# DeltaNet and MLP-Mixer on one core: the joins of 32-blocks on eight 32x32 places of TensorE instead of four

## The chip, the core and the metric

The kernel runs on one core of a Trainium2 chip. TensorE does the matmuls (PE in the profile; its weight loads are listed apart as PEld), VectorE is DVE, ScalarE is ACT, GpSimd is POOL, and SyncE (SP) issues the DMAs. TensorE takes its operands from SBUF and writes to PSUM; the copies that this text speaks of bring results from PSUM back to SBUF on ACT. The metric is the device time of one execution in microseconds (us), lower is better.

## What is computed

A DeltaNet attention over 4 batches, 8 heads, 768 positions and 48 features, then an MLP-Mixer block on its output. All in fp32.

```python
def _attn_ref(q, k, v, beta):
    k_n = k / (np.linalg.norm(k, axis=-1, keepdims=True) + 1e-06)
    state = np.zeros((B, H, D, D), dtype=np.float32)
    for t in range(S):
        kt, vt, bt = (k_n[:, :, t], v[:, :, t], beta[:, :, t, None])
        y[:, :, t] = np.einsum('bhd,bhde->bhe', q[:, :, t], state)
        v_old = np.einsum('bhde,bhd->bhe', state, kt)
        state = state + bt[:, :, :, None] * np.einsum('bhd,bhe->bhde', kt, vt - v_old)

def _moe_ref(x, w_tok1, w_tok2, w_ch1, w_ch2):
    xt = x.transpose(0, 2, 1)
    h = np.maximum(xt @ w_tok1, 0.0) @ w_tok2
    u = x + h.transpose(0, 2, 1)
    return u + np.maximum(u @ w_ch1, 0.0) @ w_ch2
```

## The kernel before

The recurrence runs over chunks of C = 64 positions. A *unit* u is 128 positions of one batch, two chunks; there are 24 units, 6 to a batch. Within a chunk the recurrence is a triangular system for each head, so the kernel makes the inverse of a 64x64 unit triangular matrix per head and chunk. A unit has 8 such pairs of matrices (`NB = 8`, index `nb = 2p + cc` for head pair `p` and chunk `cc`); each pair stands on the 128 partitions, one matrix on partitions 0 to 63 and the other on 64 to 127. They are the columns `TC` of the unit's tile `gm`.

The inverse is made in blocks of HB = 32: the two diagonal 32x32 blocks of each matrix are inverted by `invert` (on DVE, in rounds of units: 0 to 3, 4 and 5, 6 to 9, 10 to 13, 14 to 17, 18 to 21, 22 and 23; from unit 6 on the blocks go out and come back by DMA, `to_parts` and `from_parts`). The block off the diagonal is then two 32x32 products, and that is `join` (line 726):

- DVE transposes the first inverted block into `t11` (line 734).
- TensorE multiplies it with the block off the diagonal into `p_z` (line 748), ACT copies `p_z` to `zst` (line 754).
- TensorE multiplies `zst` with the second inverted block into `p_x`, and ACT copies `p_x` into `gm` (`into`, line 739).

From unit 6 on the second product of a unit is done together with the first product of the next unit of its round: that is a *double join* (lines 748 and 751, 32 matmuls in turn, four copies). The first unit of a round has the first product alone; the last one also has its own second product behind it, a *closing join* (line 767, 16 matmuls, two copies). Double joins are those of units 7, 8, 9, 11, 12, 13, 15, 16, 17, 19, 20, 21 and 23, closing ones those of units 9, 13, 17, 21 and 23 (units 0 to 5 are done one by one).

A matmul whose operands lie on 32 partitions and whose result goes to 32 partitions uses one of the array's 32x32 places: the row block is given by the operands' partitions, the column block by the result's. With

```python
halves = [(slice(r.start, r.start + HB), slice(r.start + HB, r.stop)) for r in PAR]
```

row blocks 0 and 2 feed column blocks 1 and 3 in the first product, row blocks 1 and 3 feed column blocks 0 and 2 in the second. So a double join uses four places, a closing join two. `p_z` and `p_x` are tiles of the PSUM tag "prep", which has two buffers that the grams `p_g` (line 440) and, for early units, the transposes `p_t` also take.

The chunks' recurrence is `recur`: `p_k` (line 790), `rest` on DVE (line 797), `p_y` and `p_w` in turn (lines 810 and 814; `p_w` reads the joined columns of `gm`), ACT's copy of `p_w` to `w_t` (line 820), `p_s` and `p_y` in turn (lines 828 and 829), DVE's `s_t` (line 837), ACT's two copies of `p_y` into `xb` (line 842). The MLP of a finished batch (`mixer`, `wide_fast`: `p_r`, `p_c`, `p_o`, `p_ut`, `p`, `p_h`) runs beside the recurrence of the next one; ACT and DVE empty its PSUM tiles (`r`, `u_t`, `xb`), tag "mlp" with three buffers.

What follows what is a table of words: every stage is a generator, and `order` names them one after the other (`j` for a join, `r` a step of the recurrence, `m` the MLP, `i` a step of `invert`, `c` and `d` the grams, `k`, `v`, `p` loads and preparation). Each word advances its generator to the next `yield`. On each engine the instructions run in this order. A join's steps are three words: the transpose, the matmuls, the copies.

Of the kernel before, what the change touches and what calls it, by code (L numbers as in the profile page):

```python
# [13 lines left out]
C = 64  # L14
U = 128
DP = 64
HB = 32
# [6 lines left out]
def kernel(  # L24
# [39 lines left out]
    nc = tc.nc  # L64
# [30 lines left out]
    def ps_prep(shape, name):  # L95
        return psum.tile(shape, FP32, name=name, tag="prep", bufs=2)
# [34 lines left out]
    NL = 2  # L131
# [208 lines left out]
        )  # L340

    ranked = set()
    spread = set()
    keyed = set()

# [26 lines left out]
    def load_kq(u):  # L372
        b, c = divmod(u, NCH)
        kst = kst_of[slot(u)]
        if u >= TU:
            yield from load_rows(u, 0, k)
            assert last_in(u) in ranked
            yield from stacked(kst, k, u)
            yield from load_rows(u, 1, q)
            return  # L380
        for pad, src in ((kpad, k), (qpad, q)):
            assert last_in(u) is None or (pad is kpad, last_in(u)) in turned
            nc.sync.dma_start(
                out=pad[slot(u)][:, :, 0:D],
                in_=src[b, :, c * U : (c + 1) * U, :].rearrange("h t d -> t h d"),
            )
            yield
            if src is k and u >= RU:
                yield from stacked(kst, k, u)

        heads = kpad[slot(u)].rearrange("t (p par) d -> t p par d", par=2)
        for cc in range(2 if u < RU else 0):
            for par in range(2):
                nc.scalar.copy(kst[PAR[par ^ cc], :, cc], heads[PAR[cc], :, par, 0:D])
                yield

    def stacked(dst, src, u):
# [55 lines left out]
    def prep(u):  # L453

        b, c = divmod(u, NCH)
        kst = kst_of[slot(u)]
        if u < TU:
            kp, qp = kpad[slot(u)], qpad[slot(u)]
        gm, kqt, nrm = gm_of(u), kqts[place(u)], nrms[place(u)]
        bet = beta_st[:, b, :, 2 * c : 2 * c + 2]  # L460

        ksq = work.tile([128, NB, D], FP32, name="ksq", bufs=1)
        nc.scalar.square(ksq, kst.rearrange("s p c d -> s (p c) d"))
        yield
        ksum = work.tile([128, NB], FP32, name="ksum")
        nc.vector.tensor_reduce(
            out=ksum, in_=ksq, axis=mybir.AxisListType.X, op=ALU.add
        )
        yield
        nrm_f = nrm.rearrange("s p c -> s (p c)")  # L470
        nc.scalar.sqrt(nrm_f, ksum)
        nc.scalar.activation(ksum, nrm_f, ACTF.Square, bias=eps)
        yield
        cs = work.tile([128, NP, 2], FP32, name="cs")
        nc.vector.reciprocal(ksum, ksum)
        nc.vector.tensor_tensor(
            out=cs, in0=ksum.rearrange("s (p c) -> s p c", c=2), in1=bet, op=ALU.mult
        )
        yield

        assert beta_in
        ps_turn = ps_mlp if u < NCH else ps_prep
        if u < TU:
            p_t = ps_turn([128, NP, 2, C], "p_t")
            for p in range(NP):
                nc.tensor.transpose(p_t[:, p], kp[:, 2 * p : 2 * p + 2], ident)
            turned.add((True, u))
            yield
            nc.scalar.copy(kqt[:, :, :, 0], p_t)
        else:  # L490
            assert (0, u) in spread and 2 * before_in(u) + 1 in keyed
            turn_rows(u, 0)
        yield
        mb = work.tile([128, NP, 2, C], FP32, name="mb", bufs=1)
        made[u] = mb
        scaler = nc.vector if u in EARLY_SC else nc.gpsimd
        scaler.tensor_tensor(  # L497
            out=mb, in0=mask_c[:, None, None, :].to_broadcast([128, NP, 2, C]),
            in1=cs[:, :, :, None].to_broadcast([128, NP, 2, C]), op=ALU.mult,
        )  # L500
        yield
        if u < TU:
            p_t = ps_turn([128, NP, 2, C], "p_t")
            for p in range(NP):
                nc.tensor.transpose(p_t[:, p], qp[:, 2 * p : 2 * p + 2], ident)
            turned.add((False, u))
            yield
            assert before_in(u) is None or before_in(u) in asked
            nc.scalar.copy(kqt[:, :, :, 1], p_t)  # L509
        else:  # L510
            assert (1, u) in spread and before_in(u) in asked
            turn_rows(u, 1)
        yield
        scaler.tensor_tensor(
            out=blocks(gm)[:, :, :, KC], in0=kst,
            in1=cs[:, :, :, None].to_broadcast([128, NP, 2, D]), op=ALU.mult,
        )
        ranked.add(u)
        grown.add(u)
        yield  # L520
# [206 lines left out]
    def join(u):  # L727

        done = joined_16 if u < NCH else inverted
        wt = gm_of(u)[:, :, TC]  # L730
        first = u < NCH or u == rounds[round_of[u][0]][0]
        last = u < NCH or u == rounds[round_of[u][0]][-1]
        assert done.issuperset([(u, 0), (u, 2)])
        nc.vector.transpose(t11, wt[:, :, 0:HB])
        yield

        def into(x, w):
            for r, r2 in halves:
                nc.scalar.copy(w[r, :, HB:C], x[r])

        assert len(left_over) == (not first)
        before = None if first else left_over.pop()
        assert first or done.issuperset([(before, 1), (before, 3)])
        p_z = ps_prep([128, NB, HB], "p_z")
        p_x = ps_prep([128, NB, HB], "p_x") if before else None
        for nb in range(NB):
            for r, r2 in halves:
                nc.tensor.matmul(p_z[r2, nb], wt[r, nb, HB:C], t11[r, nb])  # L748
                if before:
                    w = gm_of(before)[:, :, TC]  # L750
                    nc.tensor.matmul(p_x[r, nb], zst[r2, nb], w[r2, nb, HB:C])
        yield
        for r, r2 in halves:
            nc.scalar.copy(zst[r2], p_z[r2])
        if before:
            into(p_x, gm_of(before)[:, :, TC])
            joined.add(before)
        if not last:
            left_over.append(u)
        yield  # L760
        if not last:
            return
        assert done.issuperset([(u, 1), (u, 3)])
        p_x = ps_prep([128, NB, HB], "p_x")
        for nb in range(NB):
            for r, r2 in halves:
                nc.tensor.matmul(p_x[r, nb], zst[r2, nb], wt[r2, nb, HB:C])
        yield
        into(p_x, wt)
        joined.add(u)  # L770
        yield

# [92 lines left out]
    def sum_weights():  # L865
        def block_of(z):
            j, k = z
            for f in range(FT * j, FT * j + FT):
                piece_of(wc1, k, f * 128)
            return w_block(j, k)  # L870

        a = {(j, k): (j, k) for j in range(3) for k in range(NCB)}
        add, sub = ALU.add, ALU.subtract
        made = (
            ("w12", a[1, 2], a[0, 2], sub), ("w11", a[0, 1], "w12", add),
            ("w3", a[1, 0], a[0, 0], sub), ("w2", a[1, 1], "w3", sub),
            ("w5", a[1, 2], a[2, 0], add),
            ("w13", a[0, 2], a[2, 2], add), ("w14", "w13", "w5", sub),
            ("w1", a[0, 0], a[1, 2], sub), ("w13", a[2, 1], "w12", sub),
            ("w6", a[1, 0], a[1, 1], sub), ("w6", "w6", a[2, 0], add),  # L880
            ("w7", None, a[2, 0], sub),
            ("w15", a[2, 2], a[2, 1], sub), ("w15", "w15", a[1, 2], add),
            ("w9", a[0, 1], "w2", sub), ("w9", "w9", a[2, 1], add),
        )
        for i, (out, x, y, op) in enumerate(made):
            j = {"w13": 0, "w9": 0, "w1": 0, "w6": 1, "w7": 2, "w15": 2}.get(out)
            assert j is None or used.issuperset(range(FT * j, FT * j + FT))
            outs = sums[out]
            n = WB // len(outs)
            for h, o in enumerate(outs):  # L890
                cut = slice(h * n, h * n + n)
                p, q = (
                    sums[z][0][:, cut] if isinstance(z, str) else z and block_of(z)[:, cut]
                    for z in (x, y)
                )
                if p is None:
                    nc.vector.tensor_scalar_mul(o, q, -1.0)
                else:
                    nc.vector.tensor_tensor(out=o, in0=p, in1=q, op=op)
            if out not in [m[0] for m in made[i + 1 :]]:  # L900
                summed.add(out)
            yield
# [376 lines left out]
```

## Time and profile before

| | us |
|---|---|
| median of three timed runs | 641.43 (640.62 to 643.88) |
| the profiled execution's own time | 638.03 |
| its span in the trace | 636.3 |
| busy: PE / PEld / DVE / ACT / POOL | 606.3 / 529.0 / 447.3 / 259.5 / 108.7 |
| first product of joins, PE (L748, late units) | 16.2 in 704 records |
| second product in double joins, PE (L751) | 10.0 in 416 records |
| second product alone, PE (L767) | 6.2 in 288 records |
| copies zst<-p_z, ACT (L754) | 17.4 in 48 |
| copies gm<-p_x, ACT (L739) | 15.9 in 44 |

A row of the timeline gives the start and the length in us, the engine, the line, the operation, the tiles (out<-in), for matmuls the array's rows and columns, then the shape and the count of merged records; in square brackets stands how long the engine was idle before it and what ended that. A row of the groups gives line, engine, operation, tiles, shape and count, then busy us and mean ns of one, then the idle time before. A row of the stretches gives the busy us (and count) of PE, PEld, DVE, ACT and POOL, then TensorE's granted clock, the DMA share and GB/s. A record of a pipelined matmul lasts longer than the step from it to the next one; the steps between starts tell the pace.

### The profile page before, as it was taken

Reading aid. Unit: us, or ns where it says so; the run is one execution under the profiler, and the core shown is the slowest. Engines: PE = TensorE matmul, PEld = TensorE weight load, DVE = VectorE, ACT = ScalarE, POOL = GpSimd, SP = SyncE. Lnnn points to the kernel's source line nnn. Section 1 sums busy time; section 2 is a strip of 40 time slices with the busy share of each in tenths; the row PEclk is TensorE's granted clock in tenths of the full one; section 3 lists DMA queues with packets and bytes.
Section 4 is the critical chain, followed back from the end, with each engine's and each line's share of the span. In section 5 each row is a group of like instructions: output and inputs, shape, how many; then the busy total and the mean of one; then the engine's idle time right before and its main releaser. Section 6 shows DMA issues by size and latency. Waiting matters only on the chain.

```text
span 636.3 us, 21488 instructions
## 1 busy us (share of the span) xinstructions
PE 606.3 (95%) x9132; PEld 529.0 (83%) x9132; DVE 447.3 (70%) x1132; ACT 259.5 (41%) x631; POOL 108.7 (17%) x146
## 2 busy tenths in 40 slices
PE   8488798899999999999999999999999999999997
PEld 5367676667898988958999999769999987999997
DVE  4987876966899568988969987785627253373643
ACT  7758886447422242125623333135244230223240
POOL 2348364235301113021110010101010000000000
PEclk9878997899999999999999999999999999999999
DMA  9787568646442444354444033202020000000000
GB/s 201 131 145 170 138 133 206 151 111 155 104 111 60 92 110 92 81 131 79 92 103 101 13 94 49 66 10 38 2 54 2 27 2 0 26 1 26 1 26 26
DMA packets 135776, 50.27 MB, mean 79 GB/s; under 512 B 114656, under 2 KB 130144, under 8 KB 135680
## 3 DMA queue, kind: packets, MB, share of 16 engines
q1 hardware_dynamic: 135680, 48.89, 34.5%
q8 instruction: 72, 1.18, 0.8%
q14 instruction: 24, 0.20, 0.1%
HBM read 39.42 MB, written 9.44 MB: 77 GB/s over the span
## 4 chain that ended last, share of the span: by engine, by line
PE 81%; DVE 7%; ACT 5%; DMA 3%; issue 2%; SPq 1%; POOL 0%; DVEq 0%; ACTq 0%; POOLq 0%
PE p_o L1088 26%; PE p_r L958 19%; PE p_c L1066 7%; PE p L986 5%; PE p_h L999 5%; PE p_k L790 3%; PE p_s L828 3%; PE p_g L440 3%; PE p_y L810 3%; DMA d<-in_moe_w_ch_dram 1%; PE p_z L748 1%; PE p_ut L1009 1%; PE p_w L814 1%; DVE sub L661 1%; PE p_y L829 1%
## 5 line engine op out<-in xcount | busy, mean ns | idle before, releaser
L1088 PE MATMUL p_o<-wc,r 128*128 128x192 f32 x720 | 125.8, 329 | 0.6 <-ACT u_t L1013 0.6
L1088 PEld LDWEIGHTS p_o<-wc,r 128*128 128x128 f32 x720 | 116.7, 190 | 2.7 <-ACT u_t L1013 1.1
L970 DVE TENSOR_TENSOR r<-r,p_r 128x512 f32<-128x512 f32 x90 | 59.7, 684 | 39.9 <-PE p_r L958 38.8
L1017 DVE TENSOR_TENSOR xb<-xb,p_o 128x192 f32<-128x192 f32 x84 | 29.3, 350 | 59.5 <-PE p_o L1088 59.3
L967 ACT COPY r<-p_r 128x512 f32<-128x512 f32 x54 | 31.5, 584 | 91.4 <-PE p_r L958 89.8
L666 DVE TENSOR_TENSOR x<-x,sub 128x84 f32<-128x84 f32 (+24 forms) x178 | 59.6, 335 | 6.1
L661 DVE TENSOR_TENSOR sub<-x 128x84 f32<-128x84 f32 (+24 forms) x178 | 58.4, 328 | 7.1 <-DMA x<-n_dram 2.8
L1066 PE MATMUL p_c<-u_t,wc 128*128 128x256 f32 x216 | 51.2, 387 | 0.2 <-ACT u_t L1013 0.2
L1088 PE MATMUL p_o<-wc,s 128*128 128x192 f32 x288 | 50.5, 329 | 0.3 <-DVE xb L1017 0.3
L414 POOL TENSOR_TENSOR v_st<-v_st,nrm 128x384 f32<-128x384 f32 x24 | 20.6, 859 | 174.6 <-DMA v_st<-in_v_dram 140.7
L1088 PEld LDWEIGHTS p_o<-wc,s 128*128 128x128 f32 x288 | 46.8, 190 | 1.2 <-DVE xb L1017 0.6
L820 ACT COPY w_t<-p_w 128x192 f32<-128x192 f32 x48 | 15.3, 319 | 73.2 <-PE p_w L814 72.5
L1066 PEld LDWEIGHTS p_c<-u_t,wc 128*128 128x128 f32 x216 | 39.6, 190 | 5.9 <-ACT u_t L1013 0.4
L974 ACT ACTIVATE r<-r 128x512 f32<-128x512 f32 x54 | 33.8, 630 | 25.6 <-DVE r L970 25.3
L440 PE MATMUL p_g<-kq 48*64 48x128 f32 (+1 forms) x704 | 38.3, 290 | 3.3 <-ACT kq L509 3.3
L497 POOL TENSOR_TENSOR mb<-mask_c,cs 128x512 f32<-128x512 f32 x20 | 21.0, 1050 | 114.1 <-DVE gm L443 45.1
L842 ACT ACTIVATE xb<-p_y 64x192 f32<-64x192 f32 x96 | 31.1, 324 | 21.3 <-PE p_y L829 10.5
L958 PE MATMUL p_r<-u_t,wc 128*128 128x128 f32 x288 | 38.5, 277 | 0.0
L958 PE MATMUL p_r<-t_d,wc 128*128 128x128 f32 x288 | 37.2, 280 | 0.0
L443 DVE TENSOR_TENSOR gm<-p_g,mb 128x512 f32<-128x512 f32 x44 | 29.4, 683 | 10.0 <-PE p_g L440 7.2
L986 PE MATMUL p<-xb,w 128*128 128x384 f32 x96 | 35.6, 513 | 0.0
L958 PEld LDWEIGHTS p_r<-u_t,wc 128*128 128x128 f32 x288 | 35.3, 192 | 0.3
(177 smaller groups left out, 1200.1 us busy)
## 6 DMA issues: line engine op xcount, KB each, us to landing
d<-in_moe_w_ch_dram SPq DMA_DIRECT2D x24, 384.0 KB, 3.9
v_st<-in_v_dram SPq DMA_DIRECT2D x96, 48.0 KB, 2.5
out_dram<-xb SPq DMA_DIRECT2D x23, 192.0 KB, 1.9
kst<-in_k_dram SPq DMA_DIRECT2D x64, 48.0 KB, 3.2
n_dram<-gm SPq DMA_DIRECT2D x72, 32.0 KB, 2.4
pads<-in_k_dram SPq DMA_DIRECT2D x24, 96.0 KB, 2.4
pads<-in_q_dram SPq DMA_DIRECT2D x24, 96.0 KB, 2.5
gm<-w_dram SPq DMA_DIRECT2D x72, 32.0 KB, 2.1
```

The costliest lines, as they stand in the source:

```text
L440: nc.tensor.matmul(p_g[PAR[i ^ cc], p], kqt[f, p, cc, 0], kqt[f, p, cc])
L661: nc.vector.tensor_tensor(out=tmp, in0=y[:, :, 0:s, s : s + 1].to_broadcast([n, k, s, w]), in1=y[:, :, s : s + 1, s + 1 : m].to_broadcast( ...
L666: nc.vector.tensor_tensor(out=y[:, :, 0:s, s + 1 : m], in0=y[:, :, 0:s, s + 1 : m], in1=tmp, op=ALU.add,)
L842: nc.scalar.mul(y[:, :, D * i : D * i + D], p_y[PAR[1 - i]], 1.0 if c else -1.0)
L958: nc.tensor.matmul(p[:, i], pieces[i // width][:, at : at + 128], f[f"u{n}"], start=first and i == 0, stop=True, skip_group_check=True,)
L967: nc.scalar.copy(o, p)
L970: nc.vector.tensor_tensor(out=o, in0=o, in1=p, op=ALU.add if sign > 0 else ALU.subtract)
L974: nc.scalar.activation(o, o, ACTF.Relu)
L986: nc.tensor.matmul(p_1[dh], piece_of(w1, c, 0)[:, dh * 128 : (dh + 1) * 128], xb[:, c], start=(c == 0), stop=(c == NCH - 1),)
L999: nc.tensor.matmul(p_h, piece_of(w2, j, c * 128)[:, c * 128 : (c + 1) * 128], r1[j], start=(j == 0), stop=(j == NDH - 1),)
L1066: nc.tensor.matmul(p_c[:, k], piece_of(wc1, cb, f * 128)[:, f * 128 : (f + 1) * 128], u_t[:, cb], start=(cb == 0), stop=(cb == NCB - 1),)
L1088: nc.tensor.matmul(p, a[:, m], wc2[:, m, j], start=(start and i == 0), stop=(i == NM - 1), skip_group_check=True,)
```

## The change

From unit 6 on, double and closing joins run on twice as many places. Matrices with even `nb` go as before; for odd `nb` the result goes to the column blocks of the other half: row block 0 feeds column block 3, row block 2 feeds 1 (first product), row block 1 feeds 2 and row block 3 feeds 0 (second product). The results of even `nb` stand in one PSUM tile [128, 4, 32], those of odd `nb` in a second one; in a double join both tiles hold both products, on different partitions. The copies put each block where it belongs: for odd `nb` they read one block of 32 partitions and write another. A double join has eight copies of 32x128 instead of four of 32x256, a closing join four instead of two, and takes two "prep" buffers instead of one. The first unit of a round (6, 10, 14, 18, 22) and units 0 to 5 are as before. The other edits are assertions and the sets that they read; `order` is the same.

```diff
+        def crossed(side):
+
+            for odd, x in enumerate(both):
+                for i in range(2):
+                    yield (
+                        halves[i][side], slice(odd, NB, 2),
+                        x[halves[i ^ odd][side]],
+                    )
+
...
-        p_z = ps_prep([128, NB, HB], "p_z")
-        p_x = ps_prep([128, NB, HB], "p_x") if before else None
-        for nb in range(NB):
+        wide = u >= 6 and not first
+        if wide:
+            both = [ps_prep([128, NB // 2, HB], "p_z") for _ in range(2)]
+        else:
+            p_z = ps_prep([128, NB, HB], "p_z")
+            p_x = ps_prep([128, NB, HB], "p_x") if before else None
+        if wide:
+            for nb in range(NB):
+                for i, (r, r2) in enumerate(halves):
+                    lo, hi = halves[i ^ nb % 2]
+                    x = both[nb % 2]
+                    nc.tensor.matmul(x[hi, nb // 2], wt[r, nb, HB:C], t11[r, nb])
+                    if before:
+                        w = gm_of(before)[:, :, TC]
+                        nc.tensor.matmul(
+                            x[lo, nb // 2], zst[r2, nb], w[r2, nb, HB:C]
+                        )
+        for nb in range(0 if wide else NB):
...
-        for r, r2 in halves:
-            nc.scalar.copy(zst[r2], p_z[r2])
-        if before:
-            into(p_x, gm_of(before)[:, :, TC])
-            joined.add(before)
...
+        if wide:
+            for r, nbs, x in crossed(1):
+                nc.scalar.copy(zst[r, nbs], x)
+            if before:
+                for r, nbs, x in crossed(0):
+                    nc.scalar.copy(gm_of(before)[r, nbs, TC][:, :, HB:C], x)
+                joined.add(before)
...
-        p_x = ps_prep([128, NB, HB], "p_x")
-        for nb in range(NB):
-            for r, r2 in halves:
-                nc.tensor.matmul(p_x[r, nb], zst[r2, nb], wt[r2, nb, HB:C])
-        yield
-        into(p_x, wt)
+        wide = u >= 6
+        if wide:
+            both = [ps_prep([128, NB // 2, HB], "p_x") for _ in range(2)]
+            for nb in range(NB):
+                for i, (r, r2) in enumerate(halves):
+                    nc.tensor.matmul(
+                        both[nb % 2][halves[i ^ nb % 2][0], nb // 2],
+                        zst[r2, nb], wt[r2, nb, HB:C],
+                    )
...
+        if wide:
+            for r, nbs, x in crossed(0):
+                nc.scalar.copy(wt[r, nbs, HB:C], x)
+        else:
+            into(p_x, wt)
```

How the instructions stand on ACT at the double join of unit 12, before (an instruction with "x2" stands twice):

```order
L842 ACTIVATE xb<-p_y 64x4x48
L754 COPY zst<-p_z 32x256 [waits PE_49] x2
L739 COPY gm<-p_x 32x8x32 x2
L820 COPY w_t<-p_w 128x192 [waits PE_49,Activation_49]
L1075 ACTIVATE r_3736<-p_c 128x512 [waits PE_49]
```

and with the change (line numbers are those of the changed kernel: 909 is 842, 799 and 802 are the copies, 887 is 820, 1144 is 1075):

```order
L909 ACTIVATE xb<-p_y 64x4x48
L799 COPY zst<-p_z 32x4x32 [waits PE_49]
L799 COPY zst<-p_z 32x4x32
L799 COPY zst<-p_z 32x4x32 [waits PE_49]
L799 COPY zst<-p_z 32x4x32
L802 COPY gm<-p_z 32x4x32 x4
L887 COPY w_t<-p_w 128x192 [waits PE_49,Activation_49]
L1144 ACTIVATE r_3755<-p_c 128x512 [waits PE_49]
```

Eight copies of half the size stand where four stood; what is behind them, the copy of `w_t` first, is the same.

On PE at the closing join of unit 13, before, with the buffer numbers in the names:

```order
L1088 MATMUL p_o2_4065<-wc2_126,s1_3956 128x192 x6
L814 MATMUL p_w_4176<-v_st_3943,gm_96 64x48 x8
L767 MATMUL p_x_4187<-gm_96,zst_109 32x32 x16
L828 MATMUL p_s_4213<-w_t_111,gm_96 64x48
L829 MATMUL p_y_4175<-w_t_111,gm_96 64x48
```

and with the change (1157 is 1088, 881 is 814, 821 is the closing join, 895 is 828):

```order
L1157 MATMUL p_o2_4088<-wc2_126,s1_3979 128x192 x6
L881 MATMUL p_w_4203<-v_st_3966,gm_96 64x48 x8
L821 MATMUL p_x_4214<-gm_96,zst_109 32x32 x2
L821 MATMUL p_x_4215<-gm_96,zst_109 32x32 x2
...
L895 MATMUL p_s_4241<-w_t_111,gm_96 64x48
```

The 16 matmuls stand at the same place between `p_w` and `p_s`, in pairs that go to two tiles in turn (4214 and 4215).

More of the change, by code (lines that the diff above doesn't have):

```diff
@@ L342 @@
     ranked = set()
+    keys_in = set()
+    pads_in = set()
+    held = {"t11": None, "zst": None}
     spread = set()
@@ L377, in load_kq @@
             assert last_in(u) in ranked
-            yield from stacked(kst, k, u)
+            for n, _ in enumerate(stacked(kst, k, u)):
+                if n == 3:
+                    keys_in.add(u)
+                yield
             yield from load_rows(u, 1, q)
@@ L386, in load_kq @@
             )
+            pads_in.add((pad is kpad, u))
             yield
             if src is k and u >= RU:
-                yield from stacked(kst, k, u)
+                for n, _ in enumerate(stacked(kst, k, u)):
+                    if n == 3:
+                        keys_in.add(u)
+                    yield
         heads = kpad[slot(u)].rearrange("t (p par) d -> t p par d", par=2)
@@ L394, in load_kq @@
                 nc.scalar.copy(kst[PAR[par ^ cc], :, cc], heads[PAR[cc], :, par, 0:D])
+                if cc and par:
+                    keys_in.add(u)
                 yield
@@ L460, in prep @@
         bet = beta_st[:, b, :, 2 * c : 2 * c + 2]
+        assert u in keys_in
         ksq = work.tile([128, NB, D], FP32, name="ksq", bufs=1)
@@ L486, in prep @@
                 nc.tensor.transpose(p_t[:, p], kp[:, 2 * p : 2 * p + 2], ident)
+            assert (True, u) in pads_in
             turned.add((True, u))
@@ L505, in prep @@
                 nc.tensor.transpose(p_t[:, p], qp[:, 2 * p : 2 * p + 2], ident)
+            assert (False, u) in pads_in
             turned.add((False, u))
@@ L732, in join @@
         last = u < NCH or u == rounds[round_of[u][0]][-1]
-        assert done.issuperset([(u, 0), (u, 2)])
+        assert done.issuperset([(u, 0), (u, 2)]) and held["t11"] is None
+        held["t11"] = u
         nc.vector.transpose(t11, wt[:, :, 0:HB])
@@ L751, in join @@
                     nc.tensor.matmul(p_x[r, nb], zst[r2, nb], w[r2, nb, HB:C])
+        assert held["zst"] == before
+        held.update(t11=None, zst=None)
         yield
-        for r, r2 in halves:
-            nc.scalar.copy(zst[r2], p_z[r2])
-        if before:
-            into(p_x, gm_of(before)[:, :, TC])
-            joined.add(before)
+        assert held["zst"] is None
+        held["zst"] = u
+        if wide:
[6 more added lines that the diff above has]
+        else:
+            for r, r2 in halves:
+                nc.scalar.copy(zst[r2], p_z[r2])
+            if before:
+                into(p_x, gm_of(before)[:, :, TC])
+                joined.add(before)
         if not last:
@@ L763, in join @@
         assert done.issuperset([(u, 1), (u, 3)])
-        p_x = ps_prep([128, NB, HB], "p_x")
-        for nb in range(NB):
-            for r, r2 in halves:
-                nc.tensor.matmul(p_x[r, nb], zst[r2, nb], wt[r2, nb, HB:C])
-        yield
-        into(p_x, wt)
+        wide = u >= 6
[7 more added lines that the diff above has]
+                    )
+        else:
+            p_x = ps_prep([128, NB, HB], "p_x")
+            for nb in range(NB):
+                for r, r2 in halves:
+                    nc.tensor.matmul(p_x[r, nb], zst[r2, nb], wt[r2, nb, HB:C])
+        held["zst"] = None
+        yield
+        if wide:
+            for r, nbs, x in crossed(0):
+                nc.scalar.copy(wt[r, nbs, HB:C], x)
+        else:
+            into(p_x, wt)
         joined.add(u)
@@ L870, in block_of @@
             return w_block(j, k)
+        for u in range(NL, WIDE):
+            assert slot(u) < NL or u in ranked and turned.issuperset([(True, u), (False, u)])
         a = {(j, k): (j, k) for j in range(3) for k in range(NCB)}
```

## The prediction

> **What bounds the kernel now.** I read the page first (busy shares, the chain that ended last), then the busy time by stretches, then the timeline of PE, ACT and DVE around single joins.
>
> ```profile
> span 636.3 us, 21488 instructions
> PE 606.3 (95%) x9132; PEld 529.0 (83%) x9132; DVE 447.3 (70%) x1132; ACT 259.5 (41%) x631; POOL 108.7 (17%) x146
> PE 81%; DVE 7%; ACT 5%; DMA 3%; issue 2%; SPq 1%; POOL 0%; DVEq 0%; ACTq 0%; POOLq 0%
> ...
> 150.00:200.00 50.00, 49.99 (x766) 43.86 (x765) 44.59 (x112) 17.90 (x44) 14.56 (x18) 1.00 0.50 118
> 300.00:350.00 50.00, 49.60 (x943) 46.65 (x938) 41.59 (x102) 20.54 (x50) 6.87 (x10) 1.00 0.45 100
> ```
>
> The reader is to see that in these stretches PE is busy 49.6 and 50 of 50 us, and that the chain which ended last runs through PE for 81% of the span; ACT is idle more than half of the time. The joins that change lie between 141 and 488 us, so what PE saves in a join counts, unless the next instruction of PE then waits for another engine. DVE has 5 us free in 150 to 200 and some 8 in 300 to 350: it can follow a little, not a lot.
>
> One double join (unit 12, with what unit 11 left over) and one closing join (unit 13), PE's rows:
>
> ```profile
> 231.57 0.21 PE L748 MATMUL p_z<-t,gm 32*32 32x32 f32 x1
> ...
> 231.59 0.21 PE L751 MATMUL p_x<-gm,zst 32*32 32x32 f32 x1
> ...
> 232.13 0.19 PE L751 MATMUL p_x<-gm,zst 32*32 32x32 f32 x1
> 232.25 0.32 PE L790 MATMUL p_k<-s_t,kq 48*64 48x48 f32 x4
> ...
> 260.97 0.69 PE L767 MATMUL p_x<-gm,zst 32*32 32x32 f32 x32
> 261.60 0.25 PE L828 MATMUL p_s<-w_t,gm 64*64 64x48 f32 x1
> ```
>
> An fp32 matmul leaves two records, so the 32 matmuls of a double join are 64 records: first start 231.57, last 232.13, 0.56 us, in 16 rounds of four (one on each place), 0.035 us a round with the start in it. The closing join (L767, 16 matmuls on two places) has 32 records in 0.69 − 0.19 = 0.50 us: 16 rounds of two, 0.031 a round. Half the places, nearly the same round: a place takes a new record some 32 ns after its last, and that is what sets the length. The first four records, one on each place, follow each other by about 7 ns (231.57 to 231.59).
>
> **The change part by part.** *Double joins* (units 7, 8, 9, 11, 12, 13, 15, 16, 17, 19, 20, 21, 23: 13 of them). Eight places make rounds of eight, eight rounds: 8 × 0.032 = 0.26 us if places alone set the pace; but eight records at 7 ns take 0.053, more than 0.032, so I expect the issue to set it: 63 × 0.007 = 0.44 us against 0.56, **0.12 saved each, 1.56 in all**. Bounds: 0 (no overlap of the new places) and 0.56 − 0.28 = 0.28. I take the 7 ns, the only pace in these rows at which four free places are filled. Whether two places of one row block run beside each other is shown by a neighbour:
>
> ```profile
> 220.19 0.67 PE L790 MATMUL p_k<-s_t,kq 48*64 48x48 f32 x16
> ...
> 174.42 0.25 PE L810 MATMUL p_y<-s_t,kq 48*64 48x48 f32 x1
> ...
> 174.88 0.22 PE L814 MATMUL p_w<-rest,gm 64*64 64x48 f32 x1
> ```
>
> p_k uses two places on different rows: 16 records in 0.67 − 0.22 = 0.45 us. p_y and p_w together use four places, two on each row block, writing two banks: 32 records in 0.46 us. Twice the places, the same time, though row blocks are shared.
>
> The Trainium skill, "TensorE: Matmul & The Clock Gate", section "The mechanism", says that a weight load overlaps running matmuls only when its row group differs. That speaks against this change, whose added places all lie on row groups already in use. By it PE's gain below would be 0 instead of 2.16. The trace does not agree with the rule at 64 rows; at 32 no run here shows it.
>
> *Closing joins* (units 9, 13, 17, 21, 23) go from two places to four: 8 rounds × 0.032 = 0.26 instead of 0.50, 0.24 saved on PE. Four of the five stand between p_w and p_s as cover for ACT's copy of w_t. What is left there:
>
> ```profile
> 261.14 0.32 ACT L820 COPY w_t<-p_w 128x192 f32<-128x192 f32 x1 [1.20 <-PE p_w L814]
> ...
> 235.15 0.32 ACT L820 COPY w_t<-p_w 128x192 f32<-128x192 f32 x1 [1.23 <-PE p_w L814]
> ...
> 235.52 0.25 PE L828 MATMUL p_s<-w_t,gm 64*64 64x48 f32 x1
> ...
> 231.69 0.35 DVE L837 TENSOR_TENSOR s_t<-s_t,p_s 128x192 f32<-128x192 f32 x1 [0.71 <-PE p_y L829]
> ```
>
> p_s follows a w_t that ended at 235.47 at 235.52, 0.05 later. So in the closing join at 260.97 p_s may start at 261.46 + 0.05 = 261.51 instead of 261.60: 0.09 instead of 0.24. Four times 0.09 and once 0.24 (unit 17, with MLP work behind): **0.60**. The same wall stands behind the double join at 231.57, where p_k needs s_t, done at 232.04: it may start at 232.09, 0.16 before now, more than the 0.12 that I count. PE's gain is 1.56 + 0.60 = 2.16 us.
>
> *Copies.* Four copies of 32x256 become eight of 32x128 in a double join, two become four in a closing one: 13 × 4 + 5 × 2 = 62 more on ACT. The shape is not in the trace; the nearest are
>
> ```profile
> L717 ACT COPY gm<-p_x 16x128 f32<-16x128 f32 x16 | 4.1, 254 | 1.1 <-PE p_x L712 0.9
> ...
> 297.68 0.75 ACT L754 COPY zst<-p_z 32x256 f32<-32x256 f32 x2 [1.04 <-PE p_x L751]
> 298.45 0.75 ACT L739 COPY gm<-p_x 32x256 f32<-32x256 f32 x2
> 299.32 0.58 ACT L967 COPY r<-p_r 128x512 f32<-128x512 f32 x1
> ...
> 299.23 0.33 PE L814 MATMUL p_w<-rest,gm 64*64 64x48 f32 x4
> ```
>
> Two copies of today's shape take 0.75. 128 elements per partition cost 0.254 with 16 partitions; I take that for 32 (bounds 0.19, half of today's 0.375, and 0.375, nothing saved by the smaller size). With the 0.01 between copies that the rows show: eight take 8 × 0.265 = 2.12 us instead of 1.50, 0.62 more, of which 0.12 is regained by the earlier start: ACT is free 0.5 us later. In all 13 × 0.62 + 5 × 0.3 = 9.6 us on an engine that is idle for 377. Behind unit 12's copies the next one that PE needs (w_t at 235.15) comes after 1.23 us of idle time: nothing lost. The Trainium skill, "TensorEngine Tiling (Array Packing)", section "PSUM Bottleneck", warns of just this: tiling speeds TensorE, not the emptying of PSUM. No copy row above contradicts it; its place here is the last rival below.
>
> Where the cover is thin: at unit 15 p_w starts at 299.23 and reads the moved-back blocks of unit 14; of its even blocks the sixth copy is the last, 297.68 − 0.12 + 6 × 0.265 + 0.05 = 299.20, while PE would now come at 299.11: 0.09 lost. At unit 7:
>
> ```profile
> 144.26 0.60 ACT L1075 ACTIVATE r<-p_c 128x512 f32<-128x512 f32 x1
> ...
> 144.52 0.44 DVE L734 STREAM_TRANSPOSE t<-gm 128x256 f32<-128x256 f32 x1
> ...
> 145.01 0.24 PE L748 MATMUL p_z<-t,gm 32*32 32x32 f32 x2
> ```
>
> the next join starts behind DVE's transpose (144.96), which no shorter join brings forward: that 0.12 is lost. ACT has no gap there: the row at 144.26 shows no idle time ahead of it. For all such places together, and for what DVE can't follow, I charge one such delay of 0.5 us, between 0 and 2 (four of them). PSUM: a double join now holds its first "prep" buffer until the sixth copy (the second today) and the other until the eighth; a closing join takes two buffers instead of one. At unit 15 the next user, a p_g, comes beside the p_w at 299.23, so it waits no longer than the 0.09 already counted; elsewhere other stages of PE lie between, and I count nothing. If that cover were gone, PE would stand for what the copies grow by, 0.5 us a time, which the bound of 2 holds.
>
> **Sum.** 2.16 − 0.09 − 0.12 − 0.5 = 1.45 us, of the profiled execution's 638.03 (span 636.3 and 1.7 around it). That execution lies below the three timed ones (640.62 to 643.88, median 641.43), so I take the difference off the median: **640.0 us**, 0.2% faster, own range 639.0 to 641.3. That is within the 0.5% (3.2 us) that I take a measurement of this kernel to tell from no change.
>
> **The rivals.** *Places set the pace, not the issue* (0.15). For it: PE keeps a queue, so issue may run ahead of the places. Against: the first four records come 7 ns apart although their places are free. Then 0.28 in nine double joins, 0.15 in the four with a w_t or s_t behind them, 0.60 in the closing ones: 3.7, less the costs above, about 2.9: 638.5. The Trainium skill's span model ("TensorE: Matmul & The Clock Gate", "Measured speedup vs the span model", about 4 ns a tile) would give 64 × 4 = 0.26 us, this case; the 7 ns of the trace do not agree with it.
>
> *The new places don't overlap* (0.15): a row block takes one record at a time, whatever column block it feeds, so 16 rounds remain and the change does not do what it says. PE gains nothing; the costs of 0.1 to 1.5 us stay: 642.2. Against it stand the p_y and p_w rows.
>
> *The copies decide* (0.12), slower. ACT runs in order, so each double join pushes r evictions and w_t behind it by 0.62, or 0.5 after an earlier start. It decides wherever less than 0.5 us lies between the last copy and the next ACT result that PE awaits: unit 15 has 0.12 (299.20 to r at 299.32), unit 7 nothing, unit 12 1.23. If eight of 13 are of the first kind: 8 × 0.62 less 5 × 0.12 and 0.6 is 3.8 lost: 645.2; all 13 give 13 × 0.62 − 0.6 = 7.5, 648.9. Against: PE has other work queued behind most joins, and three "mlp" buffers to run ahead.
>
> **How the numbers follow.** Forecast 0.55, rivals 0.15, 0.15, 0.12, other 0.03. The range goes from the first rival to beyond the second with the spread of the timed runs: 637.9 to 643.4; the third lies outside. Faster by over 0.5%: half of the first rival, the rest of "other" and a little scatter, 0.13. Slower: the last rival and a little, 0.13. Same: 0.74.
>
> **What would show it.** A double join's first to last start near 0.44 us (0.28 and 0.56 for the first two rivals), a closing one near 0.26; p_s within 0.1 us behind w_t after closing joins; copies of 32x128 near 0.255 and ACT's busy time up by about 10 us; no new row of PE waiting for r or w_t above 1 us. A PE busy time that falls by less than 1 us, or new waits for ACT of more than 2, make the forecast wrong.

## The result and the profile after

| | median of the runs, us | lowest to highest | profiled execution, us (span) |
|---|---|---|---|
| before, 22 runs beside the change | 640.33 | 637.84 to 643.88 | 638.03 (636.3) |
| after, 22 runs | 640.06 | 637.62 to 643.34 | 640.08 (638.3) |

The ratio after to before is 0.9994, 95% interval 0.9978 to 1.001: between 1.4 us faster and 0.6 us slower, no change that can be told. The forecast of 640.0, "same", came out, in part by luck: it was taken off 641.43, the median of three runs of before, and the 22 runs have 640.33. A start that was 1.1 us too high met a gain that was too large by about as much. The sum behind the forecast did not come out: its main term was zero.

The page of after, with busy time, instructions and the shares of the chain that ended last:

```profile
span 638.3 us, 21546 instructions
PE 610.2 (96%) x9132; PEld 529.7 (83%) x9132; DVE 449.7 (70%) x1132; ACT 268.4 (42%) x693; POOL 109.5 (17%) x146
PE 76%; DVE 7%; ACT 6%; DMA 4%; SPq 3%; issue 3%; POOL 1%; ACTq 0%; POOLq 0%; DVEq 0%
```

PE has as many matmuls as before (9132), ACT 62 instructions and 8.9 us more. PE's busy time rose by 3.9 us, which looks like a loss in the joins and is none. The busy time by stretches shows it, before and then after (length, then PE, PEld, DVE, ACT and POOL busy, the granted clock, DMA):

```profile
0.00:140.00 140.00, 115.09 (x2340) 88.27 (x2342) 109.72 (x287) 93.89 (x249) 58.92 (x80) 0.91 0.72 152
215.00:500.00 285.00, 284.55 (x4590) 252.29 (x4589) 212.49 (x544) 99.94 (x243) 31.42 (x44) 1.00 0.29 65
```

```profile
0.00:140.00 140.00, 118.91 (x2357) 89.78 (x2358) 110.98 (x288) 94.89 (x251) 59.58 (x80) 0.91 0.72 153
215.00:500.00 285.00, 284.24 (x4591) 251.69 (x4590) 214.42 (x547) 106.85 (x291) 31.93 (x44) 1.00 0.30 65
```

The 3.8 us lie in the first 140 us, ahead of every join that changed. From 215 to 500 us, where most of them are, PE is as full as it was.

**Inside a double join.** Twelve of the 13 double joins take 562 or 563 ns from first to last start (unit 8: 665). Before it was eleven (unit 8: 1437, 0.6 us of it under "issue", where the profile shows nothing that PE waited for; unit 9: 680). Unit 8's length moves from profile to profile: with the change profiled again it is 1803. But the time is spent otherwise. The weight loads (PEld) show it best; unit 13's join before, with its 1st, 33rd and 34th load and what follows (start, duration, engine, line, operation, tiles, shape, records):

```profile
257.54 0.10 PEld L748 LDWEIGHTS p_z<-t,gm 32*32 32x32 f32 x1 [0.23 <-DVE x L666]
...
257.79 0.11 PEld L748 LDWEIGHTS p_z<-t,gm 32*32 32x32 f32 x1
257.82 0.10 PEld L751 LDWEIGHTS p_x<-gm,zst 32*32 32x32 f32 x1
257.82 0.12 PEld L748 LDWEIGHTS p_z<-t,gm 32*32 32x32 f32 x2
257.85 0.11 PEld L751 LDWEIGHTS p_x<-gm,zst 32*32 32x32 f32 x2
...
258.08 0.10 PEld L751 LDWEIGHTS p_x<-gm,zst 32*32 32x32 f32 x1
```

and the same join after:

```profile
259.94 0.10 PEld L780 LDWEIGHTS p_z<-t,gm 32*32 32x32 f32 x1 [0.23 <-DVE x L681]
259.95 0.10 PEld L783 LDWEIGHTS p_z<-gm,zst 32*32 32x32 f32 x1
...
260.07 0.11 PEld L783 LDWEIGHTS p_z<-gm,zst 32*32 32x32 f32 x1
260.19 0.10 PEld L780 LDWEIGHTS p_z<-t,gm 32*32 32x32 f32 x1
260.22 0.10 PEld L783 LDWEIGHTS p_z<-gm,zst 32*32 32x32 f32 x1
...
260.25 0.11 PEld L783 LDWEIGHTS p_z<-gm,zst 32*32 32x32 f32 x2
...
260.48 0.10 PEld L783 LDWEIGHTS p_z<-gm,zst 32*32 32x32 f32 x1
```

After, 33 loads are out within 0.13 us, and then none comes until 0.25 us after the start. Before, on four places, the 33rd load came at 0.25 (257.79). From there on the two joins are alike: a load at 0.28 after the start (257.82 and 260.22), the last at 0.54 (258.08 and 260.48). The matmuls follow, here the 32nd record, the 33rd (with the 34th) and the last:

```profile
260.10 0.19 PE L783 MATMUL p_z<-gm,zst 32*32 32x32 f32 x1
260.18 0.22 PE L780 MATMUL p_z<-t,gm 32*32 32x32 f32 x2
...
260.50 0.19 PE L783 MATMUL p_z<-gm,zst 32*32 32x32 f32 x1
```

The 33rd record starts 239 ns after the first, 76 behind the 32nd. The second half comes at two records in 0.0165 us in both kernels. So eight places do work faster than four (16 matmuls in 163 ns, before 262), but only on the first 16 matmuls of the burst. I read it so: PE has these 16 at hand when the burst begins, the other 16 arrive at a pace that the places do not set, and that was already the limit of the second half before. The loads speak for this reading. At 134 ns 33 of them had started and 27 matmul records; when the pause of the matmuls ends, still 33, beside 32 records. Had only the matmuls been held back, loads could have stayed ahead of them as they were at 134 ns, six loads ahead.

The number 16 fits a statement of the Trainium skill, "TensorE: Matmul & The Clock Gate", section "The mechanism": PE keeps a window of 64 instructions. Sixteen fp32 matmuls are 32 loads and 32 matmul records, 64 in all. The runs show the count, not the part of the chip behind it.

**The closing joins** did halve: 262 to 263 ns instead of 502 to 503, all five. ACT's `w_t` and PE's next tile at unit 13:

```profile
263.54 0.32 ACT L887 COPY w_t<-p_w 128x192 f32<-128x192 f32 x1 [0.71 <-PE p_w L881]
...
263.37 0.45 PE L821 MATMUL p_x<-gm,zst 32*32 32x32 f32 x32
263.92 0.25 PE L895 MATMUL p_s<-w_t,gm 64*64 64x48 f32 x1
```

`w_t` ends at 263.86 and `p_s` starts at 263.92, 0.55 after the join's start; before it was 261.60 − 260.97 = 0.63.

**The copies**, by line:

```profile
L799 ACT COPY zst<-p_z x52: 254/257/261, 141.7 to 476.4; 32x128 f32<-32x128 f32 x52
...
L802 ACT COPY gm<-p_z x52: 252/256/258, 142.8 to 477.5; 32x128 f32<-32x128 f32 x52
its engine sat idle before it (us, times) until:
who waited for it (us, times):
  DVE r L1039: 0.7, 1
  PEld p_w L881: 0.5, 1
  PEld p_y L877: 0.3, 1
  PEld p_g L452: 0.2, 1
```

A copy of 32x128 takes 0.257 us. Of 52 copies back into `gm`, three held up a weight load, 1.0 us in all. Only one moved PE's matmuls, at unit 15: from the join's start to `p_g` 301.60 − 299.16 = 2.44 us instead of 299.21 − 296.84 = 2.37.

Why then is the profiled execution of after 2 us longer than that of before? Matching matmul records of the two start 1.8 us earlier in after at 146 us, and 2.2 us later at 187 us. PE's waits after 130 us, after (tile and line, what it waited for; us in total, times, longest):

```profile
PE p_o L1157 <- DVE xb L1086: 2.2, 2, 1.9
PE p_o L1157 <- ACT u_t L1082: 0.6, 2, 0.3
...
```

PE stood for DVE's `xb`, and DVE's timeline says why:

```profile
177.66 1.11 DVE L369 STREAM_TRANSPOSE kq<-pads 128x512 f32<-128x512 f32 x1
181.86 0.19 DVE L676 TENSOR_TENSOR sub<-x 128x30 f32<-128x30 f32 x1 [3.08 <-DMA x<-n_dram]
...
182.19 0.35 DVE L1086 TENSOR_TENSOR xb<-xb,p_o 128x192 f32<-128x192 f32 x1
```

`sub` waits 3.08 us for a DMA, with `xb` queued behind it. Behind that wait the granted clock (the third number from the end) was 0.50 for 3.4 us:

```profile
183.80:187.20 3.40, 3.40 (x41) 2.87 (x40) 3.17 (x11) 0.32 (x1) 0.00 (x0) 0.50 0.24 59
```

The starts of `p_o` there are 320 ns apart instead of 163, and the mean clock from 140 to 215 us is 0.98, before 1.00. From 176 to 187 us the matmul records fall 3.7 us back against before, 2.1 at the wait and 1.6 under the halved clock. Whether the change causes this wait is a question for the runs below.

### The profile page after: what moved, and what is told of

The parts are those of the page before. It is cut to its first block, busy times and chain, and to the rows that moved or that the text cites. A ratio compares the mean times of both kernels' runs of the same rounds, so it can differ in the third digit from the quotient of the medians.

```text
span 638.3 us, 21546 instructions
## 1 busy us (share of the span) xinstructions
PE 610.2 (96%) x9132; PEld 529.7 (83%) x9132; DVE 449.7 (70%) x1132; ACT 268.4 (42%) x693; POOL 109.5 (17%) x146
## 4 chain that ended last, share of the span: by engine, by line
PE 76%; DVE 7%; ACT 6%; DMA 4%; SPq 3%; issue 3%; POOL 1%; ACTq 0%; POOLq 0%; DVEq 0%
PE p_o L1157 24%; PE p_r L1027 19%; PE p_c L1135 6%; PE p L1055 5%; PE p_h L1068 5%; PE p_s L895 3%; PE p_y L877 3%; PE p_k L857 3%; PE p_g L452 2%; PE p_w L881 1%; DMA d<-in_moe_w_ch_dram 1%; DMA n_dram<-gm 1%; PE p_ut L1078 1%; PE p_y L896 1%; ACT d L277 1%
## 5 line engine op out<-in xcount | busy, mean ns | idle before, releaser
L1157 PE MATMUL p_o<-wc,r 128*128 128x192 f32 x720 | 127.2, 331 | 2.5 <-DVE xb L1086 1.9
```

The source lines that it names most:

```text
L1157: nc.tensor.matmul(p, a[:, m], wc2[:, m, j], start=(start and i == 0), stop=(i == NM - 1), skip_group_check=True,)
```

## The experiments

Three theories. *Supply*: a burst finds 16 matmuls at hand, later ones come at 16.5 ns each whatever the places, so double joins gain nothing and closing joins (16 matmuls) gain all. *Pace*: eight places cannot go faster than half the 32 matmuls in 0.26 us, so the length is a matter of the places. *Copies*: the double joins do help, and the 52 more copies that they bring take it back.

### The two kinds of join apart, more copies, and the change again

Five timed rounds on one chip, with shared runs of before (35 runs, median 642.14, 638.42 to 646.7).

Only the closing joins on eight places:

```
-        wide = u >= 6 and not first
+        wide = False
```

> Only the closing joins use the new places (the changed kernel's form); the double joins are those of before, with four copies of 32x256. Theory 'supply' (a double join is held by the pace at which its matmuls past the 16th arrive, places are not its limit; the added copies are nearly free): closing joins 0.26 us from first to last start, p_s 0.05 to 0.06 us earlier behind four of them, 0.24 saved at the fifth, so about 0.45 us less than before, ratio 0.9985 to 1.0000, and the same time as the changed kernel within 0.5 us. Theory 'copies' (the 52 added copies in double joins cost what the closing joins gain): ratio to before 0.9985 to 1.0000 too, but 1 us or more below double_only of this call.

Only the double joins:

```
-        wide = u >= 6
+        wide = False
```

> Only the double joins use the new places, with eight copies; the closing joins are those of before. Theory 'supply': double joins last 0.56 us from first to last start as before, ACT has 8 us more to do, hidden; ratio 0.9985 to 1.0015. Theory 'copies': nothing gained on PE and stalls behind the copies of 0.1 us or more at each of 13 joins: ratio 1.002 to 1.010.

Two of a double join's eight copies made twice:

```
-            for r, nbs, x in crossed(1):
-                nc.scalar.copy(zst[r, nbs], x)
+            for n, (r, nbs, x) in enumerate(crossed(1)):
+                for _ in range(2 if n < 2 else 1):
+                    nc.scalar.copy(zst[r, nbs], x)
```

> The changed kernel with two of the eight copies of every double join made twice (26 more copies of 32x128 on ACT, some 0.53 us per double join, about what the change itself added). Theory 'supply': hidden like the first addition, at most 0.8 us more than the changed kernel, ratio to before 0.998 to 1.0015. Theory 'copies': 13 times up to 0.5 us, 2 to 6 us more, ratio 1.003 to 1.010.

The change as it is:

> The changed kernel once more, beside the three others on one chip. Both theories: ratio 0.998 to 1.001. In the profiled execution of the changed kernel PE stood 2.2 us for DVE near 180 us, behind the DMA that brings the blocks of invert's third round, and then ran some 4 us at half clock. If that is scatter of the DMA, it is absent or of another size here; if the change causes it, it stands at the same place with 1.5 us or more.

| kernel | runs | median, us | ratio to before, 95% | profiled span | unit 11's double join to behind the last closing join |
|---|---|---|---|---|---|
| closing joins only | 12 | 641.96 | 1.0004 [0.9975, 1.0032] | 644.1 | 268.2 |
| double joins only | 12 | 642.70 | 1.0004 [0.9976, 1.0033] | 642.3 | 268.4 |
| ten copies | 12 | 642.88 | 1.0004 [0.998, 1.0029] | 638.4 | 267.8 |
| the change again | 12 | 640.63 | 0.9981 [0.9948, 1.0015] | 645.4 | 268.3 |
| the change, first profile | 22 | 640.06 | 0.9994 [0.9978, 1.001] | 638.3 | 266.6 |
| before, first and second profile | | | | 636.3, 637.8 | 266.8, 266.9 |

None can be told from before. Nor does the table settle what the copies cost: by these intervals they could be worth up to 0.3%, and the median of ten copies lies 2.3 us above that of the change again, where *supply* allowed 0.8, in runs that scatter by 6 to 9 us. The spans of two profiles of the change (638.3 and 645.4) lie 7 us apart: a single profile's span says nothing about effects of 1 us. Here the traces say more than the times. Their joins are as *supply* has them: closing joins take 262 or 263 ns in "closing joins only" and 502 or 503 in "double joins only", and the double joins take 561 to 563 in both, but for unit 8. PE's waits from 215 to 500 us with ten copies:

```profile
PE p_g L452 <- ACT gm L803: 0.6, 1, 0.6
```

At unit 15 PE now stands 0.6 us for ACT, where it came 0.07 later with the change (0.13 with the change again). Twenty-six more copies of 0.26 us are 6.7 us on ACT: a small part arrives on PE, and the first place is the one where the prediction saw thin cover. The last column does not price the copies. Ten copies has 267.8 there against 266.6 in after, but the change again, without the added copies, has 268.3. In that profile PE waits 1.13 us for DVE's `rest`, behind an ACT that waits 1.25 us for a DMA:

```profile
247.84 0.52 ACT L476 ACTIVATE ksq<-kst 128x384 f32<-128x384 f32 x1 [1.25 <-DMA kst<-in_k_dram]
...
251.76 0.22 PE L881 MATMUL p_w<-rest,gm 64*64 64x48 f32 x1 [1.13 <-DVE rest L864]
```

"Double joins only" has the same wait. The change's own copies, 8.9 us, cost 0.07 at unit 15 and nothing else that I could find in the first profile of the change; the times alone do not bound their cost so tightly. As an account of where the 1.56 us went, *copies* falls: the double joins are not shorter on PE, so there is no gain to take back.

### A burst cut in two

In each double join one matmul of 128x128 on unused tiles is put in, so that the burst stands for a moment; what it writes is not read. First after 16 of the 32 matmuls, then after 24, and, as a control, after 16 on the four old places (with the closing joins as in the change).

```
+                if nb == 4:
+                    nc.tensor.matmul(
+                        p_warm[:, 0:1], warm[:, 0:128],
+                        warm[:, 0:128][:, None, :].to_broadcast([128, 1, 128]),
+                    )
```

> The changed kernel with one filler matmul of 128x128 between the fourth and the fifth nb of each double join, so that a join is two bursts of 16 matmuls (32 records) on eight places. Theory 'supply' (the first 16 matmuls of a burst are at hand, later ones arrive at 16.5 ns each): each burst 0.16 to 0.18 us from first to last start. Rival 'pace' (32x32 matmuls start at most once in 8 ns whatever the places): each burst 0.25 to 0.27 us.

With `nb == 6`:

> The same filler between the sixth and the seventh nb: bursts of 24 and 8 matmuls. 'Supply': the first burst 0.27 + 16 records at 8.25 ns = 0.40 us with a gap of 0.07 to 0.1 us behind its 32nd record, the second 0.08 to 0.1 us. 'Pace': 0.39 and 0.13 us without such a gap.

On four places, at the same point of the old loop:

> Control: double joins on four places as before, with the filler between the fourth and the fifth nb (closing joins as in the changed kernel). Both theories: two bursts of 0.26 us each, held by the places (32 ns for a round of four). With split_16_16 at 0.17 the places matter inside a burst of 16 matmuls; with 0.26 in both they do not.

First to last start of each part, the same at all 13 joins within 1 ns except where noted (two joins, units 12 and 23, have 194 to 196 in place of 163, one has 168 or 169):

| kernel | first part, ns | second part, ns |
|---|---|---|
| eight places, 16 and 16 | 163 | 163 |
| eight places, 24 and 8 | 429, of it 163 for the first 16 | 99 |
| four places, 16 and 16 | 262 | 262 |

Unit 13's join cut at 16, PE's rows; the 128x128 matmul is the row of `p_warm`:

```profile
260.00 0.21 PE L785 MATMUL p_z<-t,gm 32*32 32x32 f32 x1
...
260.16 0.19 PE L788 MATMUL p_z<-gm,zst 32*32 32x32 f32 x1
260.28 0.49 PE L778 MATMUL p_warm<-warm 128*128 128x128 f32 x2
260.70 0.21 PE L785 MATMUL p_z<-t,gm 32*32 32x32 f32 x1
...
260.86 0.19 PE L788 MATMUL p_z<-gm,zst 32*32 32x32 f32 x1
```

and on four places:

```profile
260.07 0.21 PE L793 MATMUL p_z<-t,gm 32*32 32x32 f32 x1
...
260.34 0.19 PE L796 MATMUL p_x<-gm,zst 32*32 32x32 f32 x1
260.46 0.49 PE L788 MATMUL p_warm<-warm 128*128 128x128 f32 x2
```

Sixteen matmuls take 0.163 us on eight places, also when they are the second half; on four places 0.262. The 16 matmuls that need 0.32 us as the second half of an uncut join (239 to 562 ns) need 0.163 once the burst has stood 0.54 us (260.16 to 260.70). With the cut at 24, the eight matmuls ahead of it still come slowly: 0.27 us for them and the gap, so that the first part takes 0.43 us where 0.40 was expected. *Supply* stands, and *pace* falls: beyond the 16th, what counts is a matmul's number in the burst, not where it runs. That does not make a faster kernel. A cut join is 0.98 us from its start to the next tile (0.70 + 0.163 + 0.12) where the uncut one is 0.68, and only work that costs 0.30 us elsewhere and fits into a cut like this one would break even.

Each of the three ran once: 642.76, 644.78 and 644.17 us (before beside them 646.05). One run is no time to compare at this size.

### The burst made twice, and before once more

Each double join's 32 matmuls are issued twice over, the second time with the same result:

```
-            for nb in range(NB):
+            for nb in [*range(NB)] * 2:
```

> Each of the 13 double joins is made twice over in a row (64 matmuls, 128 records, nothing between; the second pass writes the same values). Supply (a burst finds 16 matmuls at hand when it starts, later ones arrive at 16.5 ns each): the first 32 records take 0.163 us and the next 96 come at 16.5 ns per two, so first to last start is 0.563 + 32 x 0.0165 = 1.09 us, and records 65 to 96 take 0.26 us. Rival, results (the first 16 results go to PSUM at once and the pause behind them is PSUM taking them in, again and again): the short stretch of 0.163 comes back within the burst, which is then shorter than 1.0 us. Time: 13 x 0.53 = 6.9 us more than after, about 647 to 649.

> The kernel before, unchanged, a second profile. If the wait of PE for DVE's xb of 1.2 to 2.1 us near 180 us, which four of the profiles with more copies or other places show and the first profile of before does not, comes from the change, it is absent here too; if it is scatter of the DMA transfers in front of DVE, it may be there or not, and the spans of two profiles of one kernel differ by as much as those of before and after do (2 us and more).

In all 13 joins the 33rd record comes 239 to 240 ns after the first, as in after, and then two records come per 16.5 ns. In seven joins this goes on to the end: they take 1095 to 1097 ns, the 1.09 expected, and the short stretch does not come back within a burst. PE's rows at one of them (unit 13, started at 268.52), at the beginning of the second pass:

```profile
269.12 0.21 PE L780 MATMUL p_z<-t,gm 32*32 32x32 f32 x2
269.13 0.21 PE L783 MATMUL p_z<-gm,zst 32*32 32x32 f32 x2
269.15 0.21 PE L780 MATMUL p_z<-t,gm 32*32 32x32 f32 x2
```

So it is no pause behind each 16 results. A store for 16 results that comes free one result at a time, every 16.5 ns, would leave the same matmul rows; the loads that stop as well speak against it, and no run here excludes it. The time, 658.49 us, missed the expectation of 647 to 649. The other six joins took 1235 to 3534 ns, 6.1 us beyond 1096 together, with one gap each. For the three longest gaps PE's waits have only "issue", time in which it waited for nothing that the profile shows; that the next instructions were not there yet is my reading.

```profile
PE p_z L783 <- issue: 2.9, 2, 2.3
PE p_z L780 <- issue: 2.2, 1, 2.2
```

6.9 for the doubled matmuls and 6.1 for these, and 4.3 by which this execution is behind already at its first double join (145.01 us, in after 140.76), are 17.3 of the 18.4 us between this execution and the profiled one of after.

Before, profiled again, took 639.54 us (span 637.8), and PE's waits from 150 to 215 us have the row that was in question:

```profile
PE p_o L1088 <- DVE xb L1017: 0.8, 1, 0.8
```

and on DVE the same DMA ahead of it:

```profile
182.54 0.19 DVE L661 TENSOR_TENSOR sub<-x 128x30 f32<-128x30 f32 x1 [1.99 <-DMA x<-n_dram]
```

Its records fall 1.0 us back there against the first profile of before, at the same place where after lost more. The change with ten copies, the three cut kernels and the doubled burst have no such row in that stretch. So the wait near 180 us belongs to when a DMA lands, with the change or without it. The halved clock behind it belongs to one profile: in the change again a wait of 2.1 us stands at the same place, and the clock stays at 1.00 behind it. Whether the wait is a little more frequent with the change (four of nine profiles with the change or a part of it had 1.2 us or more, one of the four without any change in its double joins, and neither of two of before) can't be told from so few.

## Why the prediction was right, and where its sum was not

- **Double joins, 13 × 0.12 = 1.56 us: wrong, 0.** The step that failed is "I expect the issue to set it: 63 × 0.007". The pace of the first four records was carried over to all 64. For the first 32 it is even too slow (31 steps in 163 ns, 5.3 each); for the second 32 it does not hold at all. The trace of before had the row against it: its first half goes in rounds of four (steps of 7, 6, 7 and 12 ns), its second in pairs (15 and 1 or 2 ns). The pace is nearly the same, 32 or 33 ns for four, but I would expect a limit by places alone to have kept the rounds. The quoted bound, "0 (no overlap of the new places)", held the value for the wrong reason.
- **Closing joins, 0.60 us: 0.50.** PE's part was right (262 instead of 0.26), and so was the wall of `w_t`: `p_s` follows it by 0.06. Unit 13 saves 0.08, units 9, 21 and 23 0.06 each, unit 17, with no wall behind it, 0.24.
- **Copies, 0.254 us each and 9.6 us more on ACT: right.** 0.257 and 8.9.
- **Unit 15, 0.09 lost: right in place and kind**, 0.07 (0.13 with the change again), by the PSUM buffer that `p_g` waits for. Unit 7's 0.12 had nothing to lose.
- **The charge of 0.5 for thin cover: too high**, as far as the first profile of the change shows it: PE has no other wait for these copies there. With ten copies the same place gives 0.6 at once, so the cover ends just behind the change's amount.
- **The sum.** −1.45 forecast; the measured terms give −0.50 + 0.07 = −0.43, and the runs −0.27 with an interval of −1.4 to +0.6. Too large a gain and too large a charge partly cancelled, what was left was under what can be told, and the 640.0 itself was met because the three runs that it starts from lie high (641.43 against 640.33). That a kernel with a main term of zero lands on the forecast is luck.
- **The rivals.** *Places set the pace* was right for the closing joins, where the forecast said the same. For the double joins it has the wrong length (0.28), and their first 16 matmuls fit neither rule: 163 ns, where four rounds of 0.032 are 128 ns and 31 steps of 7 ns are 217. *The new places don't overlap* would have priced the double joins right and is wrong: a closing join now has two places on each of two row blocks and takes half as long. The Trainium skill's rule that a weight load overlaps only across row groups ("TensorE: Matmul & The Clock Gate", "The mechanism") is contradicted by 502 to 262 ns at 32 rows. *Copies decide* did not come.
- **The signs to watch.** "A PE busy time that falls by less than 1 us" was a poor one: PE's busy time rose by 3.9 us through the first 140 us, and would have condemned any forecast. The joins' own lengths were the sign that decided.

What stays open is which part of PE sets the 16.5 ns per matmul beyond the 16th. The runs show that it is the same on four places and on eight, holds for 48 matmuls in a row, and that the fast stretch is back once the burst has stood for 0.54 us.

## What to carry to other kernels

Spreading these 32x32 matmuls over more places helped the first 16 fp32 matmuls of a burst (64 instructions with their weight loads); a longer burst ran on at 16.5 ns per matmul on four places as on eight. So look at the second half of a burst before pricing it by the first records. Price a step on PE to the next thing that PE waits for: the closing joins saved 240 ns each and kept 60 to 80 where a copy stood behind them. A change of 0.1% must be read from its own rows; the span of one profile moved by 7 us without any change.

## What the runs showed of the hardware that was not expected

- After 32 weight loads and 32 matmul records in a burst (163 ns on eight places of 32x32), the 33rd comes 239 ns after the first, and the rest at two records per 16.5 ns, with the same offsets before and after the change.
- Bursts of 128 records had a gap of 0.11 to 2.4 us in six of 13 joins, the longest under "issue" in the profile; with 64 records, before had a join of 1437 ns in place of 563.
- Two 32x32 places on one row block run beside each other at full pace: 16 fp32 matmuls in 262 ns on four places, two per row block, against 502 on two.
- A copy from PSUM of 32x128 takes 257 ns, one of 32x256 took 364: halving the elements takes off 107 ns, so the part that does not depend on size is about 150 ns, an estimate from these two sizes. That half of them end on other partitions costs nothing visible (254 to 261 ns for all 52).
